# A linear-attention and GeGLU block on one core: output weights kept by head group, their packed copy made through DRAM on ScalarE's queue, and an epsilon column

## The chip, the cores and the metric

The kernel runs on one core of a Trainium2 chip. A core has five engines that take their instructions in order: TensorE (PE; its weight loads are shown apart, as PEld), VectorE (DVE), ScalarE (ACT), GpSimd (POOL) and SyncE (SP). Sixteen DMA engines move the data; an engine that issues a transfer puts it on its own queue, here SP's (q1 in the profile) and ACT's (q10). PE writes into PSUM, which has 8 banks of 128 x 512 f32.

The metric is the device time of one execution in microseconds (us). The kernel before takes 190.47 us, the median of 3 runs (190.45 to 190.97).

## The reference

The input x has 2048 tokens of D = 448. Linear attention with H = 16 heads of 28 is followed by a GeGLU with FF = 1792, both behind a layer norm without weights and with a residual:

```python
phi = lambda t: where(t > 0, t + 1, exp(t)) + 1e-6
q, k, v = split(layernorm(x) @ wqkv)          # 16 heads of 28
pq, pk  = phi(q), phi(k)
kv  = einsum("bhsd,bhse->bhde", pk, v)        # one 28 x 28 matrix for a head
z   = einsum("bhsd->bhd", pk)
den = einsum("bhqd,bhd->bhq", pq, z) + 1e-6
o   = einsum("bhqd,bhde->bhqe", pq, kv) / den[..., None]
h   = x + o @ wo
out = h + (gelu(layernorm(h) @ w_gate) * (layernorm(h) @ w_up)) @ w_down
```

All inputs and the output are bf16; gelu is the tanh form.

## The kernel before

**Tiles and stages.** The tokens are 16 tiles of 128, or 8 pairs of tiles. The stages, with their lines of the kernel before:

1. Layer norm of each tile (`xnn`), transposed to `xnT`: tiles 0 to 3 on PE, tiles 4 to 15 by DMA transposes `xT_4` to `xT_15` that SP issues (L455).
2. Projections `k_t` and `q_t`, 4 matmuls of 128x448 each (L469). For K: exp on ACT (`ek`, L480), phi on DVE, and sums over the tokens of phi(k) with the normed x (`pt`, L488). For Q: `eq_t` (exp, L496) and `rq_t` (relu, L497) on ACT, both reading the PSUM bank of the projection. Four PSUM banks go round for the projections, so a projection can start when the fourth projection before it has been read by both.
3. `kv` (16 matmuls, L527): the 448 x 448 matrix phi(k)^T v, of which a DVE operation (`kvm`, L531) keeps the 16 diagonal blocks of 28 x 28. The heads lie in 4 groups of 4 (112 channels). `w2_0` to `w2_3` (7 matmuls, L547) multiply this block-diagonal matrix with `wo`, so that the whole of attention behind phi(q) becomes one multiplication by `w2`, 448 x 448. The results are copied out by ACT (`evwA`) and DVE (`evwD`).
4. For each pair of tiles: phi(q) (`cq`, `aq`), `t1` = phi(q) times z (POOL), the sum over each head (`dr`, DVE), plus epsilon (`deA` for tiles 0 to 3, L574; `deP` for the later pairs, L588; ACT), reciprocal, and `pn`, the scaled phi(q). Pair 0 is transposed by PE (`tro`, L599) and copied by ACT (`evo_0`, `evo_1`, L602), pairs 1 to 7 by DMA transposes `oT_p` of SP (L605).
5. `out` = transposed phi(q) times `w2`. Pair 0 takes 4 matmuls a tile (`out1_0`, `out1_1`, L617). Pairs 1 to 7 run in two parts, `outA_p` and `outB_p` (L627, L628), as 7 steps, each of two matmuls of 64 rows that work side by side on two row halves of PE. One of the two needs `w2` with its row halves swapped: `w2s`, made by two transfers SBUF to SBUF, `dws0` and `dws1`, of 168 KB each, that SP issues.
6. Residual (`hr`, L633), layer norm (`ln2`, `rstd2`, on ACT for tiles 0 and 1) and `hn`, transposed by PE for pair 0 (`trh_0`, `trh_1`, L654, copied by ACT in `evhA_0`, L658, and by DVE), for later pairs by SP's DMA transposes.
7. `gu`: gate and up products (L731, L733), again 64 rows on each half of PE side by side. Tiles 0 and 1 go as 7 groups `gu2_0` to `gu2_6` of twice 256 columns, tiles 2 and 3 as `gu2_7` to `gu2_13`; tiles 4 to 15 go four at a time. The result of gate lies in PSUM banks 0 and 1 in turn, that of up in banks 6 and 7: `gu2_v` can start when gelu (`ge0`, `ge1`, ACT, L751) and the product (`hm0`, `hm1`, DVE, L753) of group v-2 have read theirs. Both work in halves of 256.
8. `down` (L697), the last residual, and the output.

ACT reads its functions from tables: exp, ln and relu from one, gelu from another. The kernel loads the second, `tbl2` (L762), behind the last exp, relu, ln and the copy `evhA_0`, and ahead of the first `ge`.

**What sets the order.** Every operation is put down as a task with the buffers that it reads and writes; from these come the waits. For each engine a row of the table `ORDERS` lists its tasks by number, and the engine issues them in just this order. A task whose wait isn't over holds up all that stands behind it on the same engine, a DMA issue too. A second table, `HOLD`, only says which of a task's waits stands first.

The gate and up weights come in four loads of SP, `dwg0`, `dwu0`, `dwg1`, `dwu1`, behind `xT_15`; the last of them is 64 x 7 x 1024, 896 KB.

## Time and profile before

| | |
|---|---|
| median of 3 runs | 190.47 us (190.45 to 190.97) |
| span of the profiled execution | 188.3 us |
| instructions | 4459 |
| granted PE clock | 1.000 |
| busy: PE, DVE, ACT, POOL | 184.3, 129.3, 76.5, 50.0 us |
| `kv` on PE | 35.96 to 36.99 us |
| load of the gelu table on ACT | 51.12 to 52.40 us |

How the views are to be read: the first part of the profile gives the busy time of each engine. A timeline row has the start, the length, the engine, the line, the operation, out<-in and its shape and a count of instructions that are taken together; a count of 2 on a row spans both and the gap between them. A row of windows has the start and end of a stretch, its length, the busy time and count of instructions of PE, PEld, DVE, ACT and POOL, the granted clock of PE, the share of the DMA engines' time, and GB/s. A row of waits has who waits, for what, the time in us, how often and the longest. Rows of DMA queues give packets, MB and the share of 16 engines' time. Times are us from the start of the span.

### The profile page before, as it was taken

Reading aid. Unit: us, or ns where it says so; the run is one execution under the profiler, and the core shown is the slowest. Engines: PE = TensorE matmul, PEld = TensorE weight load, DVE = VectorE, ACT = ScalarE, POOL = GpSimd, SP = SyncE. Lnnn points to the kernel's source line nnn. Section 1 sums busy time; section 2 is a strip of 40 time slices with the busy share of each in tenths; the row PEclk is TensorE's granted clock in tenths of the full one; section 3 lists DMA queues with packets and bytes.
Section 4 is the critical chain, followed back from the end, with each engine's and each line's share of the span. In section 5 each row is a group of like instructions: output and inputs, shape, how many; then the busy total and the mean of one; then the engine's idle time right before and its main releaser. Section 6 shows DMA issues by size and latency. Waiting matters only on the chain.

```text
span 188.3 us, 4459 instructions
## 1 busy us (share of the span) xinstructions
PE 184.3 (98%) x1813; PEld 109.2 (58%) x1813; DVE 129.3 (69%) x330; ACT 76.5 (41%) x220; POOL 50.0 (27%) x91
## 2 busy tenths in 40 slices
...
GB/s 169 387 231 88 96 104 194 218 222 174 65 320 64 95 52 116 84 52 0 0 3 98 144 54 0 0 3 2 3 135 111 3 0 24 3 0 98 3 79 140
DMA packets 35076, 17.11 MB, mean 91 GB/s; under 512 B 26864, under 2 KB 33648, under 8 KB 35056
## 3 DMA queue, kind: packets, MB, share of 16 engines
...
q10 hardware_dynamic: 624, 0.52, 0.8%
q8 instruction: 14, 0.23, 0.5%
q14 instruction: 6, 0.05, 0.1%
...
## 4 chain that ended last, share of the span: by engine, by line
PE 94%; DVE 3%; DMA 1%; issue 0%
PE ps L733 38%; PE ps L697 19%; PE ps L469 12%; PE ps L731 9%; PE ps L488 6%; PE ps L627 3%; PE ps L678 3%; PE ps L628 2%; DMA x_sb<-in_A_x_dram 1%; DVE st L413 1%; PE ps L617 1%; PE ps L547 1%; PE ps L527 1%; PE ps L443 0%; PE ps L654 0%; DVE den L572 0%
## 5 line engine op out<-in xcount | busy, mean ns | idle before, releaser
L733 PE MATMUL ps<-hnT,wgu_sb 64*128 64x512 bf16 (+1 forms) x490 | 88.8, 333 | 0.0
L731 PE MATMUL ps<-hnT,wgu_sb 64*128 64x512 bf16 (+1 forms) x490 | 88.6, 333 | 0.0
L751 ACT ACTIVATE gl<-ps 128x256 bf16<-128x256 f32 x112 | 36.6, 383 | 85.3 <-PE ps L731 84.4
L753 DVE TENSOR_TENSOR hh<-ps,gl 128x256 bf16<-128x256 f32 x112 | 42.1, 416 | 41.4 <-ACT gl L751 41.3
L733 PEld LDWEIGHTS ps<-hnT,wgu_sb 64*128 64x128 bf16 x490 | 45.2, 94 | 32.9 <-DVE hh L753 3.4
L731 PEld LDWEIGHTS ps<-hnT,wgu_sb 64*128 64x128 bf16 x490 | 45.4, 94 | 2.5
L697 PE MATMUL ps<-wd_sb,hh 64*128 64x448 bf16 x392 | 41.5, 349 | 0.0
L697 PEld LDWEIGHTS ps<-wd_sb,hh 64*128 64x128 bf16 x392 | 23.2, 94 | 14.5
L469 PE MATMUL ps<-wqk_sb,xnT 128*128 128x448 bf16 x128 | 27.4, 353 | 0.0
L413 DVE BATCH_NORM_STATS2 st<-x_sb 128x6 f32<-128x448 bf16 x32 | 19.2, 612 | 1.8 <-DMA x_sb<-in_A_x_dram 1.7
L585 POOL TENSOR_TENSOR t<-pq,zbc 128x448 f32<-128x448 bf16 x12 | 12.3, 1042 | 23.7 <-DVE pq L583 22.0
L469 PEld LDWEIGHTS ps<-wqk_sb,xnT 128*128 128x128 bf16 x128 | 11.9, 98 | 11.4 <-DVE pk L482 0.8
L488 PE MATMUL ps<-pk,xnn 128*128 128x448 bf16 x64 | 13.9, 352 | 0.0
L627 PE MATMUL ps<-w,pqnT 64*128 64x448 bf16 x49 | 11.5, 349 | 0.1
L425 POOL TENSOR_SCALAR ln<-mv 128x2 f32<-128x2 f32 x7 | 2.0, 291 | 35.2 <-DVE mv L414 35.0
L480 ACT ACTIVATE e<-ps 128x448 bf16<-128x448 f32 x16 | 8.5, 539 | 5.6 <-PE ps L469 5.5
L628 PE MATMUL ps<-pt_sb,pqnT 64*128 64x448 bf16 x42 | 10.2, 350 | 0.0
L633 DVE TENSOR_TENSOR x_sb<-ps,x_sb 128x448 bf16<-128x448 f32 x16 | 9.6, 616 | 0.7 <-PE ps L628 0.6
L662 POOL TENSOR_SCALAR hn<-x_sb,nm,rs 128x448 bf16<-128x448 bf16 x14 | 9.9, 719 | 0.4
L482 DVE SCALAR_TENSOR_TENSOR pk<-ps,e 128x448 bf16<-128x448 f32 x16 | 9.8, 617 | 0.1
L488 PEld LDWEIGHTS ps<-pk,xnn 128*128 128x128 bf16 x64 | 6.3, 98 | 5.9 <-DVE pk L482 0.3
L453 POOL TENSOR_SCALAR xnn<-x_sb,nm,rs 128x448 bf16<-128x448 bf16 x12 | 8.9, 744 | 2.2 <-ACT rs L422 1.9
...
## 6 DMA issues: line engine op xcount, KB each, us to landing
...
wgu_sb<-in_B_w_gate_dram SPq DMA_DIRECT2D x1, 896.0 KB, 12.1
wgu_sb<-in_B_w_up_dram SPq DMA_DIRECT2D x1, 896.0 KB, 16.5
...
```

The costliest lines, as they stand in the source:

```text
L413: op("dve", lambda e: e.bn_stats(st[:, t, :], src_ap), [b_src], [b_st[t]], "bnst%s_%d" % (tag, t))
L469: ins = e.matmul(ps[:, bk, 0:D], xnT[:, t, k, :], wqk_sb[:, k, c0:c0 + D], start=(k == 0), stop=(k == 3))
L488: ins = e.matmul(ps[:, BK_PT[c], 0:D], xnn[:, t % XN_R, c * 128:(c + 1) * 128], pk[:, ip, :], start=(t == 0), stop=(t == T - 1))
L585: op("pool", lambda e, n=n: e.tensor_tensor(t1[:, n, :], pq[:, a + n, :], zbc[:, :], ALU.mult), [b_pq[a + n]] + b_z, [b_t1[n]], "t1p_%d" % ...
L627: e.matmul(ps[:, BK_OUT[0], 0:D], pqnT[ra, i2, sg // 2, :], w2[ra, sg // 2, :], start=(sg == 0), stop=(sg == 5))
L628: ins = e.matmul(ps[:, BK_OUT[1], 0:D], pqnT[rb, i2, 3 + (sg + 1) // 2, :], (w2 if sg == 6 else w2s)[rb, sg // 2, :], start=(sg == 0), sto ...
L662: op("pool", lambda e, t=t, sh=sh: e.tensor_scalar(hn[:, sh, 0:D], x_sb[:, t, :], nm2[:, t:t + 1], rs2[:, t:t + 1], ALU.add, ALU.mult), [b ...
L697: ins = e.matmul(ps[:, bko[half][n], 0:D], hh[rows, j, sl[n]], wd_sb[rows, j, :], start=(j == 0 and (half == 0 or p == 6)), stop=(j == NJ ...
L731: first = e.matmul(psG[:, jj * N:(jj + 1) * N], wgu_sb[A_, k, j * 128:(j + 1) * 128], hnT[A_, ka_, c0:c0 + N], start=(k == 0), stop=(k == ...
L733: ins = e.matmul(psU[:, jj * N:(jj + 1) * N], wgu_sb[B_, k, j * 128:(j + 1) * 128], hnT[B_, kb_, c0:c0 + N], start=(k == 0), stop=(k == NK ...
L751: G.add("act", lambda e, gi=gi, cs_=cs_, psG=psG: e.activation(gl[:, gi, cs_], psG[:, cs_], AF.Gelu_apprx_tanh), r=[b_ps[BK_G[i]]], w=[b_g ...
L753: op("dve", lambda e, dst=dst, srcU=srcU, srcL=srcL: e.tensor_tensor(dst, srcU, srcL, ALU.mult), [b_ps[BK_U[i]], b_glh], [b_ar[j_][t % HR] ...
```

## The change

- `dwo`, the load of `wo`, stands on SP's queue behind `xT_5`, no longer ahead of `xT_4`.
- The block-diagonal matrix and its product are kept by head group: `w2g` has 112 rows in 4 groups, and `w2` takes 4 matmuls of 112x448 instead of 7 (after: L607). The zeroing of the wide buffer on POOL and the copy `kvd` on DVE (L536) are gone; the unused columns of `pqn` are zeroed by POOL for pair 1 too.
- Pair 1 is done as pair 0: `out1_2` and `out1_3`, 4 matmuls a tile (after: L675), in place of `outA_1` and `outB_1`. `oT_1` transposes 8 blocks of 128 instead of 7.
- Pairs 2 to 7 still run in two packed parts. Their weights `w2p` are a copy of `w2g` in which both row halves hold all of it. It is made through DRAM by three transfers of ScalarE's queue (after: L417): `dw2w` writes `w2g` to DRAM (`w_bounce`, 112x4x448, 392 KB), and `dw2r0` and `dw2r1` read it into the two row halves (64x7x448 each, 392 KB each, in the space of `pt_sb` and `wv_sb`). `dws0` and `dws1` are gone from SP.
- `t1` gets a 29th column per head that holds epsilon, so that the sum over 29 gives the denominator with epsilon. The 4 `deA` and 6 `deP` on ACT are gone.
- For each of the 14 groups `gu2`, gelu and product are one instruction of 512 columns (`geW`, `hmW`).
- `trh` waits for the two parts of `hn` apart.
- `ORDERS` and `HOLD` are new; of each a line stands in the diff.

On ACT, around the first layer norm behind attention: before, from `eq_11`,

```order
L496 ACTIVATE eq<-ps 128x448
L420 ACTIVATE ln<-mv,eps_t 128x1 x2
L422 ACTIVATE rs<-ln 128x1 x2
L497 ACTIVATE pq<-ps 128x448
L588 ACTIVATE den<-den,eps_d 128x32
L497 ACTIVATE pq<-ps 128x448
L496 ACTIVATE eq<-ps 128x448 x2
L497 ACTIVATE pq<-ps 128x448
L496 ACTIVATE eq<-ps 128x448
L658 ACTIVATE hnT<-ps 128x7x128
```

and now, also from `eq_11`; the two DMA rows are `dw2r0` and `dw2r1` (`pv_sb` holds `w2p`), and `rq_10` is the first `pq` row:

```order
L567 ACTIVATE eq<-ps 128x448
L491 ACTIVATE ln<-mv,eps_t 128x1
L417 DMA pv_sb<-w_bounce 64x7x448
L567 ACTIVATE eq<-ps 128x448
L493 ACTIVATE rs<-ln 128x1
L568 ACTIVATE pq<-ps 128x448
L491 ACTIVATE ln<-mv,eps_t 128x1
L493 ACTIVATE rs<-ln 128x1
L417 DMA pv_sb<-w_bounce 64x7x448
L568 ACTIVATE pq<-ps 128x448
L567 ACTIVATE eq<-ps 128x448
L717 ACTIVATE hnT<-ps 128x7x128
```

Two DMA issues have come in, `eq_10` and `rq_10` stand behind the first of them, and the epsilon row is gone. The write `dw2w` stands further ahead on the same engine, behind the copies of `w2` and `eq_7`:

```order
L568 ACTIVATE pq<-ps 128x448 x2
L610 ACTIVATE w2g<-ps 112x448 x2
L567 ACTIVATE eq<-ps 128x448
L417 DMA w_bounce<-w2g 112x4x448
L567 ACTIVATE eq<-ps 128x448
L660 ACTIVATE pqnT<-ps 128x512
```

On PE from `kv` to the transposes of the second layer norm: before,

```order
L527 MATMUL ps<-pt_sb,wv_sb 112x112 x16
L469 MATMUL ps<-wqk_sb,xnT 128x448 x8
L547 MATMUL ps<-wo_sb,hh 128x448 x6
L469 MATMUL ps<-wqk_sb,xnT 128x448 x4
L547 MATMUL ps<-wo_sb,hh 128x448
L599 MATMUL ps<-ident,pqn 128x128 x8
L469 MATMUL ps<-wqk_sb,xnT 128x448 x4
L617 MATMUL ps<-w,pqnT 128x448 x8
L469 MATMUL ps<-wqk_sb,xnT 128x448 x24
L654 MATMUL ps<-ident,hn 128x128 x14
```

and now:

```order
L598 MATMUL ps<-pv_sb 112x112 x16
L540 MATMUL ps<-wqk_sb,xnT 128x448 x4
L607 MATMUL ps<-wo_sb,hh 112x448 x4
L540 MATMUL ps<-wqk_sb,xnT 128x448 x4
L657 MATMUL ps<-ident,pqn 128x128 x4
L540 MATMUL ps<-wqk_sb,xnT 128x448 x8
L657 MATMUL ps<-ident,pqn 128x128 x4
L675 MATMUL ps<-w2g,pqnT 128x448 x4
L540 MATMUL ps<-wqk_sb,xnT 128x448 x4
L675 MATMUL ps<-w2g,pqnT 128x448 x4
L540 MATMUL ps<-wqk_sb,xnT 128x448 x20
L713 MATMUL ps<-ident,hn 128x128 x14
```

One projection (4 matmuls, `q_7`) instead of two stands between `kv` and `w2`, and the transposes and output products of pair 0 are spread among the projections. The last projections are now, in this order, `q_12`, `q_10`, `q_13`, `q_15`, `q_14`.

The diff, cut to what the tasks do:

```diff
--- before.py
+++ after.py
...
-    " 168 179 192 180 346 193 205 218 307 219 206 234 308 347 235 250 251 349 309 290 289 310 311 313 293 315 317"
+    " 167 168 179 192 180 344 193 205 218 307 219 206 234 308 345 235 250 251 347 309 290 289 310 311 293 313 314"
...
-    66: (36,), 141: (140,), 165: (164,), 214: (213,), 216: (215,), 323: (302,), 326: (324,), 431: (340,), 704:
+    435: (434,), 436: (435,), 437: (433,), 438: (437,), 439: (438,), 440: (436,), 441: (440,), 442: (441,),
...
-        wv_sb = sb("wv_sb", [128, 4, D], BF16)
+        pv_sb = sb("pv_sb", [128, 8, D], BF16)
+        pt_sb, wv_sb, w2p = pv_sb[:, 0:4, :], pv_sb[:, 4:8, :], pv_sb[:, 0:NK, :]
...
-        pt_sb = sb("pt_sb", [128, 4, D], BF16)
         zbc = sb("zbc", [128, D], F32)
-        w2 = sb("w2", [128, 4, D], BF16)
-        t1 = sb("t1", [128, 2, D], F32)
+        w2g = sb("w2g", [GW, NG, D], BF16)
+        w2d = nc.dram_tensor("w2_bounce", [D, D], BF16)
+        t1 = sb("t1", [128, 2, H, DH + 1], F32)
         den = sb("den", [128, 4, H], F32)
-        eps_d = sb("eps_d", [128, 1], F32)
...
-        kvz = hh[0:GW, 6:9, :].rearrange("p a b -> p (a b)")
-        w2s = pt_sb[:, 0:3, :]
+        t1f = t1[:].rearrange("p n h d -> p n (h d)")[:, :, 0:D]
+        kvz = hh[0:GW, 6, 0:D]
...
-        dma_x("sp", 12, 16)
+        tx12 = dma_x("sp", 12, 16)
         dma_w3("sp", wv_sb, 2 * D, 3 * D, b_wv, "dwv")
         dma_w1("sp", wv_sb, 2 * D, 3 * D, b_wv, "dwv_t")
         two = dma("sp", wo_sb[:, :, :], A_wo.rearrange("(g p) n -> p g n", p=GW), [b_wo], "dwo")
...
-        op("pool", lambda e: e.memset(eps_d[:], EPS), [], [b_epsd], "epsd")
+        op("pool", lambda e: e.memset(t1[:, :, :, DH:DH + 1], EPS), [], [b_epsd], "epsd")
...
-        op("pool", lambda e: e.memset(pqn[:, 0, :].rearrange("p (n c) -> p n c", n=2)[:, :, D:512], 0.0), [], b_pqn[0], "pqnpad")
-        op("pool", lambda e: e.memset(kvz[:, GW:15 * GW], 0.0), [], [b_kvm], "kvzpad")
+        for i_ in range(2):
+            op("pool", lambda e, i_=i_: e.memset(pqn[:, i_, :].rearrange("p (n g c) -> p n g c", n=2, g=NG)[:, :, :, GW:128], 0.0), [], b_pqn[i_], "pqnpad_%d" % i_)
...
-                G.add("sp", lambda e: e.dma_start_transpose(xnT[:, t, :, :], xnn[:, i, :]), r=[b_xn[i], b_ones2], w=b_xnT[t], name="xT_%d" % t, kind="dma", after=[two])
+                G.add("sp", lambda e: e.dma_start_transpose(xnT[:, t, :, :], xnn[:, i, :]), r=[b_xn[i], b_ones2], w=b_xnT[t], name="xT_%d" % t, kind="dma", after=[tx12])
...
-        for c in range(4):
-            def fw2(e, c=c):
-                gs = (c, c + 1) if c < 3 else (3,)
-                ins = None
-                for g in gs:
-                    ins = e.matmul(ps[:, BK_W2[c], 0:D], kvc(g, c), wo_sb[:, g, :], start=(g == gs[0]), stop=(g == gs[-1]))
-                return ins
-            G.add("pe", fw2, r=[b_kvm, b_wo] + ([b_kvd] if c == 3 else []), w=[b_ps[BK_W2[c]]], name="w2_%d" % c)
...
+        for g in range(NG):
+            G.add("pe", lambda e, g=g: e.matmul(ps[0:GW, BK_W2[g], 0:D], kvz[:, g * GW:(g + 1) * GW], wo_sb[:, g, :], start=True, stop=True),
+                  r=[b_kvm, b_wo], w=[b_ps[BK_W2[g]]], name="w2_%d" % g)
+            if g % 2 == 0:
...
-        for h, (to, of) in enumerate(((A_, B_), (B_, A_))):
-            dma("sp", w2s[to, :, :], w2[of, 0:3, :], [b_w2s[h]], "dws%d" % h, r=b_w2[0:3], after=xts[-1:])
+                op("dve", lambda e, g=g: e.tensor_copy(w2g[:, g, :], ps[0:GW, BK_W2[g], 0:D]), [b_ps[BK_W2[g]]], [b_w2[g]], "evwD_%d" % g)
+        dma("act", w2d.ap().rearrange("(g p) n -> p g n", p=GW), w2g[:, :, :], [b_w2d], "dw2w", r=b_w2)
+        for h, rows in enumerate((A_, B_)):
+            dma("act", w2p[rows, :, :], w2d.ap().rearrange("(k p) n -> p k n", p=64), [b_w2p[h]], "dw2r%d" % h, r=[b_w2d])
...
-                    op(eng, lambda e, t=t, n=n: e.tensor_tensor(t1[:, n, :], pq[:, t, :], zbc[:, :], ALU.mult), [b_pq[t]] + b_z, [b_t1[n]], "t1%s_%d" % (eng[0], t))
+                    op(eng, lambda e, t=t, n=n: e.tensor_tensor(t1[:, n, :, 0:DH], pq[:, t, :].rearrange("p (h d) -> p h d", h=H), zbc[:, :].rearrange("p (h d) -> p h d", h=H), ALU.mult), [b_pq[t]] + b_z, [b_t1[n]], "t1%s_%d" % (eng[0], t))
...
-                    op("dve", lambda e, n=n, i=i: e.tensor_reduce(den[:, i, :], t1[:, n, :].rearrange("p (h d) -> p h d", h=H), AX.X, ALU.add),
-                       [b_t1[n]], [b_den[i]], "dr_%d" % t)
-                    op("act", lambda e, i=i: e.activation(den[:, i, :], den[:, i, :], AF.Identity, bias=eps_d[:, 0:1]), [b_den[i], b_epsd], [b_den[i]], "deA_%d" % t)
+                    op("dve", lambda e, n=n, i=i: e.tensor_reduce(den[:, i, :], t1[:, n, :, :], AX.X, ALU.add),
+                       [b_t1[n], b_epsd], [b_den[i]], "dr_%d" % t)
...
-                    op("dve", lambda e, t=t, n=n, i=i, i2=i2: e.tensor_tensor(
-                        pqn[:, i2, n * pst:n * pst + D].rearrange("p (h d) -> p h d", h=H), pq[:, t, :].rearrange("p (h d) -> p h d", h=H),
-                        rd[:, i, :].unsqueeze(2).to_broadcast([128, H, DH]), ALU.mult),
+                    dst = pqn[:, i2, n * 512:n * 512 + 512].rearrange("p (g c) -> p g c", g=NG)[:, :, 0:GW]
+                    op("dve", lambda e, t=t, i=i, dst=dst: e.tensor_tensor(
+                        dst.rearrange("p g (h d) -> p g h d", d=DH), pq[:, t, :].rearrange("p (g h d) -> p g h d", g=NG, d=DH),
+                        rd[:, i, :].rearrange("p (g h) -> p g h", g=NG).unsqueeze(3).to_broadcast([128, NG, 4, DH]), ALU.mult),
                        [b_pq[t], b_rd[i]], [b_pqn[i2][n]], "pn_%d" % t)
...
-                op("dve", lambda e: e.tensor_reduce(den[:, i:i + 2, :].rearrange("p n h -> p (n h)"), t1[:, :, :].rearrange("p n (h d) -> p (n h) d", h=H), AX.X, ALU.add),
-                   b_t1, b_den[i:i + 2], "drP_%d" % p)
-                op("act", lambda e: e.activation(den[:, i:i + 2, :], den[:, i:i + 2, :], AF.Identity, bias=eps_d[:, 0:1]), b_den[i:i + 2] + [b_epsd], b_den[i:i + 2], "deP_%d" % p)
+                    op("pool", lambda e, n=n: e.tensor_tensor(t1[:, n, :, 0:DH], pq[:, a + n, :].rearrange("p (h d) -> p h d", h=H), zbc[:, :].rearrange("p (h d) -> p h d", h=H), ALU.mult), [b_pq[a + n]] + b_z, [b_t1[n]], "t1p_%d" % (a + n))
+                op("dve", lambda e: e.tensor_reduce(den[:, i:i + 2, :].rearrange("p n h -> p (n h)"), t1[:, :, :, :].rearrange("p n h d -> p (n h) d"), AX.X, ALU.add),
+                   b_t1 + [b_epsd], b_den[i:i + 2], "drP_%d" % p)
...
-                G.add("sp", lambda e, i2=i2: e.dma_start_transpose(pqnT[:, i2, 0:NK, :], pqn[:, i2, 0:2 * D]),
+                G.add("sp", lambda e, i2=i2: e.dma_start_transpose(pqnT[:, i2, 0:8 if p == 1 else NK, :], pqn[:, i2, 0:1024 if p == 1 else 2 * D]),
...
-            if p == 0:
+            if p < 2:
...
-                            e.matmul(ps[:, BK_OUT[0], 0:D], pqnT[ra, i2, sg // 2, :], w2[ra, sg // 2, :], start=(sg == 0), stop=(sg == 5))
-                            ins = e.matmul(ps[:, BK_OUT[1], 0:D], pqnT[rb, i2, 3 + (sg + 1) // 2, :], (w2 if sg == 6 else w2s)[rb, sg // 2, :], start=(sg == 0), stop=(sg == 5))
+                            e.matmul(ps[:, BK_OUT[0], 0:D], pqnT[ra, i2, sg // 2, :], w2p[ra, sg, :], start=(sg == 0), stop=(sg == 5))
+                            ins = e.matmul(ps[:, BK_OUT[1], 0:D], pqnT[rb, i2, 3 + (sg + 1) // 2, :], w2p[rb, sg, :], start=(sg == 0), stop=(sg == 5))
                         return ins
-                    parts.append(G.add("pe", foutp, r=b_pqnT[i2] + b_w2 + b_w2s, w=[b_ps[b_] for b_ in BK_OUT], name="out%s_%d" % (part, p), sync=parts[-1:]))
+                    parts.append(G.add("pe", foutp, r=b_pqnT[i2] + b_w2p, w=[b_ps[b_] for b_ in BK_OUT], name="out%s_%d" % (part, p), sync=parts[-1:]))
...
+                        for m, k in enumerate((0, 1, 2, 4, 5, 6, 3)):
+                            W(m)
...
+                    G.add("pe", ftrh, r=[(b_hn[sh], 0), (b_hnd[sh], 6), (b_ident, 0)], w=[(b_ps[BK_TH[t]], 0)], name="trh_%d" % t, mw=True)
...
-                for hh_ in range(2):
-                    cs_ = slice(hh_ * 256, (hh_ + 1) * 256)
+                for hh_ in range(2 if nj == 1 else 1):
+                    cs_ = slice(hh_ * 256, (hh_ + 1) * 256) if nj == 1 else slice(0, 512)
...
-                    b_glh = b_gl2[gi][hh_]
+                    b_glh = b_gl2[gi][hh_:] if nj > 1 else b_gl2[gi][hh_:hh_ + 1]
                     G.add("act", lambda e, gi=gi, cs_=cs_, psG=psG: e.activation(gl[:, gi, cs_], psG[:, cs_], AF.Gelu_apprx_tanh),
-                          r=[b_ps[BK_G[i]]], w=[b_glh], name="ge%d_%d" % (hh_, v), after=[tbl2])
+                          r=[b_ps[BK_G[i]]], w=b_glh, name="ge%s%d_%d" % ("W" if nj > 1 else "", hh_, v), after=[tbl2])
                     op("dve", lambda e, dst=dst, srcU=srcU, srcL=srcL: e.tensor_tensor(dst, srcU, srcL, ALU.mult),
-                       [b_ps[BK_U[i]], b_glh], [b_ar[j_][t % HR] for j_ in jr for t in th], "hm%d_%d" % (hh_, v))
+                       [b_ps[BK_U[i]]] + b_glh, [b_ar[j_][t % HR] for j_ in jr for t in th], "hm%s%d_%d" % ("W" if nj > 1 else "", hh_, v))
```

31 lines of the change are left out of this document (9 added, 22 removed), and 130 rows, old and new, of tables (HOLD, ORDERS).

## The prediction

> **What bounds the kernel now.** I read the page first: the busy times, then the chain of work that ended last.
>
> ```profile
> span 188.3 us, 4459 instructions
> PE 184.3 (98%) x1813; PEld 109.2 (58%) x1813; DVE 129.3 (69%) x330; ACT 76.5 (41%) x220; POOL 50.0 (27%) x91
> ...
> PE 94%; DVE 3%; DMA 1%; issue 0%
> ```
>
> PE is busy for 184.3 of 188.3 us, so the end moves by two things only: PE work that is added or taken away, and stretches in which PE waits. The profiled span of 188.3 us stands 2.2 us under the median of 190.47; I make the sum as a difference on the span's times and add it to the median.
>
> Next I read the windows around the change, since the busy share of ACT over the whole span (41%) hides one stage. A row has start and end, length, busy time and count of PE, PEld, DVE, ACT and POOL, clock, DMA share, GB/s.
>
> ```profile
> 35.40:52.40 17.00, 16.88 (x152) 10.16 (x152) 16.28 (x38) 16.55 (x40) 6.88 (x8) 1.00 0.87 167
> 54.00:66.00 12.00, 12.00 (x190) 9.86 (x189) 11.87 (x33) 3.35 (x11) 6.10 (x10) 1.00 0.52 130
> ```
>
> From 35.4 to 52.4 us ACT is busy for 16.55 of 17.00 us: there it has no room, and PE (16.88) has none either. From 54 us on ACT has plenty, and PE is gapless. So what the change does to the time is settled by one handover, which the timelines show (ACT, then DVE, then PE):
>
> ```profile
> 45.39 0.49 ACT L420 ACTIVATE ln<-mv,eps_t 128x1 f32<-128x1 f32 x2
> ...
> 46.02 0.53 ACT L497 ACTIVATE pq<-ps 128x448 bf16<-128x448 f32 x1
> 46.45 0.31 ACT L588 ACTIVATE den<-den,eps_d 128x32 f32<-128x32 f32 x1
> 46.66 0.53 ACT L497 ACTIVATE pq<-ps 128x448 bf16<-128x448 f32 x1
> ...
> 48.84 0.95 ACT L658 ACTIVATE hnT<-ps 128x896 bf16<-128x896 bf16 x1
> ...
> 51.12 1.28 ACT L762 ACT_TABLE_LOAD   x1
> 52.41 0.66 ACT L751 ACTIVATE gl<-ps 128x256 bf16<-128x256 f32 x2
> ...
> 53.10 0.76 DVE L753 TENSOR_TENSOR hh<-ps,gl 128x256 bf16<-128x256 f32 x2
> ...
> 53.95 0.27 PE L733 MATMUL ps<-hnT,wgu_sb 64*128 64x256 bf16 x1
> ```
>
> ACT runs without a gap through the last projections to the gelu table; gelu starts at 52.41, the product ends at 53.86, and `gu2_2`, which needs that PSUM bank, starts at 53.95. ACT's chain is therefore just in time: whatever makes the table load later makes `gu2_2` later, and everything behind it. In the new order `outB_2` stands ahead of `gu2_2`, 3 packed steps of 0.19 (49.56 to 50.14 in the PE rows below). The same place in the program is then 53.95 + 0.57 = 54.52 us; that is the mark against which I measure.
>
> **The change: PE's work.** The rows are PE's, with one DVE row among them.
>
> ```profile
> 34.23 1.68 PE L469 MATMUL ps<-wqk_sb,xnT 128*128 128x448 bf16 x8
> 35.96 1.03 PE L527 MATMUL ps<-pt_sb,wv_sb 128*112 128x112 bf16 x16
> 36.83 1.68 PE L469 MATMUL ps<-wqk_sb,xnT 128*128 128x448 bf16 x8
> 37.19 0.61 DVE L531 TENSOR_TENSOR hh<-ps,mask 112x448 bf16<-112x448 f32 x1
> 38.34 1.30 PE L547 MATMUL ps<-wo_sb,hh 112*128 112x448 bf16 x6
> ...
> 47.69 0.94 PE L654 MATMUL ps<-ident,hn 128*128 128x128 bf16 x14
> ...
> 49.14 0.35 PE L627 MATMUL ps<-w,pqnT 64*128 64x448 bf16 x1
> 49.56 0.36 PE L627 MATMUL ps<-w,pqnT 64*128 64x448 bf16 x1
> ...
> 50.14 0.27 PE L733 MATMUL ps<-hnT,wgu_sb 64*128 64x256 bf16 x1
> ...
> 51.67 0.27 PE L733 MATMUL ps<-hnT,wgu_sb 64*128 64x256 bf16 x1
> ```
>
> Eight projection matmuls take from 36.83 to 38.34, 0.19 each; the lengths overlap. Three `w2` matmuls fall out: -0.57. Pair 1 goes from 7 packed steps of 0.19 to 8 matmuls of 0.19: +0.19. Sum -0.38. The gap between 49.14 and 49.56, 0.42 instead of 0.19, is a wait of 0.23 of `outB_1` that can vanish with it. Against that, `kvm` ends at 37.80 and only `q_7` (0.76, to 37.59) now covers it, not two projections: PE waits 0.2 to 0.3. PE alone therefore stands at -0.6 to -0.1. This counts only if ACT isn't the later one.
>
> **ACT's work.** Four `deA` and one `deP` ahead of the table load fall out. One takes 0.21 of ACT's time (46.45 to 46.66, where the next starts): -1.05. The five later `deP` lie in ACT's idle time, nothing. Three DMA issues come in. ACT's own issues in this trace are at the start, and the one with as many rows as the new ones (448 of 896 bytes) is SP's load of `wo`:
>
> ```profile
> 0.80 0.42 ACTq L346 DMA_DIRECT2D x_sb<-in_A_x_dram  x1
> 1.25 1.01 ACTq L346 DMA_DIRECT2D wqk_sb<-in_A_wqkv_dram  x2
> 5.50 0.59 SPq L346 DMA_DIRECT2D wo_sb<-in_A_wo_dram  x1
> ```
>
> So 0.42 to 0.6 each; I take 0.6, by the like size: +1.8. The merged gelu and product are priced from 256 and 448 columns of the same engines:
>
> ```profile
> L751 ACT ACTIVATE gl<-ps 128x256 bf16<-128x256 f32 x112 | 36.6, 383 | 85.3 <-PE ps L731 84.4
> L753 DVE TENSOR_TENSOR hh<-ps,gl 128x256 bf16<-128x256 f32 x112 | 42.1, 416 | 41.4 <-ACT gl L751 41.3
> L480 ACT ACTIVATE e<-ps 128x448 bf16<-128x448 f32 x16 | 8.5, 539 | 5.6 <-PE ps L469 5.5
> L482 DVE SCALAR_TENSOR_TENSOR pk<-ps,e 128x448 bf16<-128x448 f32 x16 | 9.8, 617 | 0.1
> ```
>
> ACT: 0.539 + 64/192 of 0.156 = 0.59; DVE: 0.617 + 64/192 of 0.201 = 0.68. With 0.1 for the handovers, 1.4 us from the table to `gu2_2`, against 1.54 before: -0.15. In steady state one bank's round is 1.4 to 1.55 against 1.53 for the other bank's group (50.14 to 51.67), so small waits of 0.1 in all may come; DVE's saving is hidden by PE. Without any wait ACT's chain would so come out at -1.05 + 1.8 - 0.15 = +0.6 against 53.95, that is 54.55, as good as the mark.
>
> **The wait that is added.** `dw2r0` reads what `dw2w` has written, so ACT stands at its issue until the write has landed, and behind it stand `eq_10`, `rstd2_0`, `rq_10`, the whole rest of the exp stage, and the table. PE waits too: `q_14` uses the PSUM bank of `q_10`. DVE waits for `rstd2` in `hn`, and `pnP_2` and SP's `oT_2` stand behind that. The question is when `dw2w` lands.
>
> `dw2w` is issued once the copies of `w2` are done, about 40 us (before: SP issues `dws0`, which waits for the same copies, at 40.37). At that time the DMA engines are full with the last weights:
>
> ```profile
> 29.33 0.76 SPq L346 DMA_DIRECT2D wgu_sb<-in_B_w_up_dram  x1
> wgu_sb<-in_B_w_up_dram SPq DMA_DIRECT2D x1, 896.0 KB, 16.5
> 40.37 1.16 SPq L346 DMA_DIRECT2D pt_sb<-w  x2
> pt_sb<-w SPq DMA_DIRECT2D x2, 168.0 KB, 5.7
> ...
> q1 hardware_dynamic: 318, 0.65, 105.4%
> ```
>
> The last load lands at 29.33 + 16.5 = 45.8; the last row (stretch 40 to 43 us) shows all 16 engines busy with SP's queue. The two copies `dws`, on that same queue, took 5.7 us and landed at 46.1 to 46.5. Would ACT's queue be served sooner? The start of the kernel has both queues loaded at once; the first two rows are 3.7 to 4.6 us, the last two 4.6 to 5.3:
>
> ```profile
> q10 hardware_dynamic: 317, 0.28, 89.8%
> q1 hardware_dynamic: 45, 0.05, 17.1%
> ...
> q1 hardware_dynamic: 238, 0.21, 87.1%
> q10 hardware_dynamic: 69, 0.05, 21.3%
> ```
>
> There ACT's load (q10, issued 1.25) moves almost alone, and then SP's (q1, issued later) almost alone: the transfers go nearly whole, in the order of issue. By this `dw2w` comes behind the last load. `dws`, 336 KB, ended 0.7 after it; 392 KB take 0.82: landing at L = 46.65. Ends: 42.1 if ACT's queue goes first (about 40 us, 0.6 for the issue, 1.05 at the rate of the start, 0.5 for the landing), and 47.3 if the write runs into `oT_1` as well. I take 46.65, since it rests on the nearest rows, same time and same kind.
>
> ACT reaches `dw2r0` at: before's 45.39 - 0.84 (`deA`) + 0.6 (`dw2w`) - 0.43 (`eq_10`, `rq_10` moved behind, `rq_11` ahead) + 0.16 (`ln2_0`; two `ln` and two `rs` take 45.39 to 46.02) = 44.9. It waits 1.75 us.
>
> From L the chain to the table's end is: `dw2r0` 0.6, `eq_10` 0.43 (46.02 to 46.45), `rstd2_0` 0.16, `rq_10` 0.43, `ln2_1` and `rstd2_1` 0.32, `dw2r1` 0.6, `rq_15` and `eq_15` 0.86, `evhA_0` 0.85 (0.95 less the 0.1 by which such rows overlap), six more of `eq` and `rq` 2.58, table 1.29 (51.12 to 52.41): 8.1. Plus 1.4: `gu2_2` at L + 9.5. PE's own chain from there is as long: `q_14` at L + 1.7, then 0.76, `trh` 0.88 (47.69 to 49.14 less three steps), 8 x 0.19, two groups 3.06, 7 x 0.19: L + 9.25. So the change is L + 9.5 - 54.52 = L - 45.0, with L = 46.65 some +1.65 us, and from then on all of PE is later by this: 190.47 + 1.65 = **192.1 us**. What PE saves lies ahead of this wait, or beside it, and is lost in it.
>
> Small things: the load of `wo` behind `xT_5` lets two transposes leave earlier by its issue (0.59) and the ten others up to as much later, -0.6 to +0.6 if PE stood on them throughout; PE's busy share leaves little for that, and I take nothing. POOL loses one zeroing and gains one, far ahead; nothing. `dw2r0` and `dw2r1` have from about 47 and 49 to 54 us, enough for 392 KB; `wd`, 1568 KB, is issued behind `oT_2` and so behind both.
>
> **A rule against the rows.** The start-up windows above show transfers nearly whole, in order of issue. The Trainium skill, "DMA: Bandwidth & Descriptors", section "Queues, rings and completion order", says that each DMA engine takes turns between the queues for which it has work, a packet of some 9 to 17 descriptors at a time. By that rule, as an estimate, `dw2w` (28 rows an engine) would need two or three turns, each behind one of the 28 rows an engine of the last load, and land well ahead of that load's end or just with it.
>
> **The rivals.**
>
> 1. The two queues take turns. In 3.7 to 4.6 us SP's queue still moved 45 packets beside ACT's 317, which speaks a little for it. `dw2w` then shares the engines with the last load, whose 0.9 MB take 4.2 us at the 0.65 MB in 3 us of the row above. Two turns of half of that, from 40 us, plus 1.05 for itself put L at 45.3 (one turn and the landing: 44; end of the load: 46.2): L - 45.0 = +0.3, 190.8.
> 2. `dw2w` is in time. ACT's queue is served at once, L = 42.1, below the 44.9 at which ACT comes; no wait, the chain is at 54.55: no change, 190.5.
> 3. Faster. As 2, and an issue costs ACT 0.42, not 0.6: then ACT's chain ends at 54.0, PE is the later one, and its -0.6 to -0.1 show; with the 0.2 that PE waits ahead of `kv` (34.23 + 8 x 0.19 to 35.96) at most -0.8: 189.7 to 190.4, taken as 189.8. It decides from L under 44.9 and issues under 0.45 each. Against it stand the 5.7 us of `dws` in the same stretch.
> 4. The change does other than it says: the wait of `trh`, the later `xT_6` or the weights of `outA_2` cost more than I see, with `dw2w` in time: up to +1, 191.3.
>
> **How the numbers follow.** Stuck behind the last load 0.55 (192.1; L from 46.0 to 47.3 gives 191.5 to 192.8, and with 0.3 for small waits in the merged groups 193.1); turns 0.17, half of it within the bound; in time without effect 0.13; faster 0.12; other 0.03. What this measurement can tell from no change is about 0.3%, 0.57 us: faster is under 189.90, slower over 191.04. So faster 0.12, same 0.13 + 0.09 = 0.22, slower 0.55 + 0.08 + 0.03 = 0.66. The range of 8 in 10 reaches from 190.1, with the turns and most of the no-wait case in it, to 193.1; the likeliest case alone has 191.5 to 193.1.
>
> **What would show it.** In the profile after: ACT idle ahead of `dw2r0` or of `eq_10`, about 44.9 to 46.7, put down to the transfer into `w_bounce`; that transfer's landing, 6 to 7 us after its issue; a PE wait of 1 us or more at `q_14`; the table load at about L + 6.8 = 53.5 instead of 51.12; gapless PE from `gu2_3` on. I'm wrong if `w_bounce` lands by 44.9, or if the table load starts by 52, or if PE waits anew further back, at `outA_2` or in the groups with the merged gelu.

## The result and the profile after

The changed kernel takes 192.48 us (median of 6 runs, 192.06 to 193.45), the kernel before 190.75 us beside it (190.45 to 190.97). The ratio is 1.0096, 95% interval 1.0076 to 1.0117: about 1.8 us slower. The ratios and times of the experiments below leave out eight executions, in four of the runs, that had a granted clock of 0.983 to 0.991 and took over 1.5% more than the fastest of their kernel.

The page of the changed kernel:

```profile
span 190.9 us, 4399 instructions
PE 184.8 (97%) x1804; PEld 113.0 (59%) x1804; DVE 128.8 (67%) x315; ACT 73.2 (38%) x196; POOL 49.6 (26%) x91
...
PE 81%; DVE 9%; DMA 7%; SPq 1%; ACT 1%; issue 0%; ACTq 0%
```

ACT has lost 3.3 us of work and DVE 0.5, and neither helps: PE is still the one that is always busy. But of the chain that ended last PE now makes up 81%, not 94%; 13% have gone to DVE, DMA and ACT. That is the form that new waits of PE take in the chain. The profiled execution of the changed kernel took 192.61 us, 1.7 us more than its span. In 58 executions of the kernel before that were run beside the experiments, the time was 1.93 to 2.06 us more than the span, and those with a span of 188.3 took 190.28 to 190.33. So by estimate the execution of before that was profiled took about 190.3, some 0.4 less than the median of before. (Why the changed kernel has 0.2 us less outside its span isn't shown.) So the two spans differ by 2.6 us where the medians differ by 1.7; the events in the traces are to be compared with that in mind.

The chain of the changed kernel (start, length, what), in the stretch of the handover:

```profile
39.99 1.17 DVE w2g L612 x2
41.18 6.34 DMA w_bounce<-w2g
...
47.55 0.62 ACTq L417
...
48.22 0.54 ACT eq L567
...
49.34 0.93 PE ps L540 x4
```

This is the wait that was added, read in one go: the copies of `w2g` end, `dw2w` is issued at 41.18 and lands 6.34 us later, at 47.52; only then ACT issues `dw2r0` (47.55), then come `eq_10` and `rq_10`, and only then PE starts `q_14`. The timelines of ACT, DVE and PE for the same place:

```profile
46.48 0.29 ACT L491 ACTIVATE ln<-mv,eps_t 128x1 f32<-128x1 f32 x1 [0.33 <-DVE mv L485]
47.55 0.62 ACTq L417 DMA_DIRECT2D pv_sb<-w_bounce  x1
48.22 0.54 ACT L567 ACTIVATE eq<-ps 128x448 bf16<-128x448 f32 x1 [1.44 <-PE ps L540]
...
54.56 1.28 ACT L821 ACT_TABLE_LOAD   x1
55.85 1.08 ACT L810 ACTIVATE gl<-ps 128x512 bf16<-128x512 f32 x2
...
56.48 0.69 DVE L812 TENSOR_TENSOR hh<-ps,gl 128x512 bf16<-128x512 f32 x1 [0.36 <-ACT gl L810]
...
57.13 0.27 PE L790 MATMUL ps<-hnT,wgu_sb 64*128 64x256 bf16 x1
```

One row can mislead: ACT's 1.44 us of idle time ahead of `eq_10` are put down to PE (L540). `q_10` was done at about 46.8 (PE starts its last projections at 45.17 with `q_12`, then `q_10`, 0.76 each). The time is `dw2r0`'s: ACT ended `ln2_0` at 46.77, stood until 47.55, and took 0.62 for the issue, which isn't counted as busy. The waits of PE name the right one:

```profile
PEld ps L540 <- ACT pq L568: 1.4, 1, 1.4
...
PEld ps L607 <- DVE hh L602: 0.9, 1, 0.9
```

The second of these is the wait for `kvm`. The table load stands at 54.56, where before had it at 51.12, and `gu2_2` starts at 57.13, where the mark of the prediction was 54.52: 2.6 us later, the whole difference of the spans. From there on the two kernels run alike.

Two places ahead of the handover have changed too. First the load of `wo` on SP's queue; the first two rows are SP's timeline, the third is the DMA issue of `xT_6` with its time to landing (4.1 us in the kernel before), the last is PE's `k_6`:

```profile
13.45 0.58 SPq L417 DMA_DIRECT2D wo_sb<-in_A_wo_dram  x1
14.09 14.46 SPq L526 DMA_TRANSPOSE xnT<-xnn  x10
...
xnT<-xnn SPq DMA_TRANSPOSE x1, 4.6
...
18.84 0.92 PE L540 MATMUL ps<-wqk_sb,xnT 128*128 128x448 bf16 x4 [0.59 <-DVE mv L485]
```

`xT_6` is issued at 14.09 and lands at 18.7, and `k_6` starts at 18.84. (The row names a DVE operation; `k_6` waits for `xT_6` and for `pk_4`, and `pk_4` was over.) From 14.09 on SP issues transposes without a gap: `xT_15` is issued 1.3 us later than before, the last weight load 1.3 us later (30.64, not 29.33), and `kv` starts at 37.12, not 35.96. Not all of that is the load's: `xT_4`, which stands ahead of it, is issued 0.5 us later already (10.81, not 10.31); in the other runs it is issued at 10.32 to 10.69, wherever `wo` stands.

Second, `kvm`, in the rows of PE and DVE:

```profile
37.12 0.99 PE L598 MATMUL ps<-pv_sb 128*112 128x112 bf16 x16
37.95 0.92 PE L540 MATMUL ps<-wqk_sb,xnT 128*128 128x448 bf16 x4
39.37 0.96 PE L607 MATMUL ps<-wo_sb,hh 112*112 112x448 bf16 x4 [0.50 <-DVE hh L602]
...
37.88 0.91 DVE L635 TENSOR_TENSOR pqn<-pq,rd 128x448 bf16<-128x448 bf16 x1
38.70 0.61 DVE L602 TENSOR_TENSOR hh<-ps,mask 112x448 bf16<-112x448 f32 x1
```

`kv` is done at 38.1, but DVE is in `pn_0` until 38.79 and does `kvm` behind it; PE is through with `q_7` at 38.7 and starts `w2` at 39.37, 0.67 us later than without a wait.

### The profile page after: what moved, and what is told of

It is laid out like the page before. It is cut to its first block, busy times and chain, and to the rows that moved or that the text cites. A ratio compares the mean times of both kernels' runs of the same rounds, so it can differ in the third digit from the quotient of the medians.

```text
span 190.9 us, 4399 instructions
## 1 busy us (share of the span) xinstructions
PE 184.8 (97%) x1804; PEld 113.0 (59%) x1804; DVE 128.8 (67%) x315; ACT 73.2 (38%) x196; POOL 49.6 (26%) x91
## 4 chain that ended last, share of the span: by engine, by line
PE 81%; DVE 9%; DMA 7%; SPq 1%; ACT 1%; issue 0%; ACTq 0%
PE ps L792 40%; PE ps L756 19%; PE ps L790 6%; PE ps L540 5%; PE ps L559 4%; DMA w_bounce<-w2g 3%; DMA x_sb<-in_A_x_dram 3%; PE ps L737 3%; DVE st L484 3%; PE ps L685 2%; PE ps L686 1%; DVE pk L553 1%; PE ps L675 1%; SPq L417 1%; DVE w2g L612 1%; DVE e L552 1%
## 5 line engine op out<-in xcount | busy, mean ns | idle before, releaser
L810 ACT ACTIVATE gl<-ps 128x256 bf16<-128x256 f32 (+1 forms) x98 | 35.3, 414 | 87.1 <-PE ps L790 86.2
L812 DVE TENSOR_TENSOR hh<-ps,gl 128x256 bf16<-128x256 f32 (+1 forms) x98 | 41.0, 455 | 40.7 <-ACT gl L810 40.7
L790 PEld LDWEIGHTS ps<-hnT,wgu_sb 64*128 64x128 bf16 x490 | 45.2, 94 | 2.8 <-ACT eq L567 0.4
L756 PEld LDWEIGHTS ps<-wd_sb,hh 64*128 64x128 bf16 x392 | 25.5, 94 | 12.1
L540 PE MATMUL ps<-wqk_sb,xnT 128*128 128x448 bf16 x128 | 28.1, 353 | 1.8 <-ACT pq L568 1.0
L540 PEld LDWEIGHTS ps<-wqk_sb,xnT 128*128 128x128 bf16 x128 | 11.9, 98 | 14.2 <-ACT pq L568 1.4
L644 POOL TENSOR_TENSOR t<-pq,zbc 128x448 f32<-128x448 bf16 x12 | 12.9, 1090 | 27.0 <-DVE pq L642 27.0
L721 POOL TENSOR_SCALAR hn<-x_sb,nm,rs 128x448 bf16<-128x448 bf16 x14 | 10.8, 780 | 0.5
L685 PE MATMUL ps<-pv_sb,pqnT 64*128 64x448 bf16 x42 | 9.9, 349 | 0.1
L686 PE MATMUL ps<-pv_sb,pqnT 64*128 64x448 bf16 x42 | 9.9, 349 | 0.0
```

The source lines that it names most:

```text
L540: ins = e.matmul(ps[:, bk, 0:D], xnT[:, t, k, :], wqk_sb[:, k, c0:c0 + D], start=(k == 0), stop=(k == 3))
L644: op("pool", lambda e, n=n: e.tensor_tensor(t1[:, n, :, 0:DH], pq[:, a + n, :].rearrange("p (h d) -> p h d", h=H), zbc[:, :].rearrange("p ...
L685: e.matmul(ps[:, BK_OUT[0], 0:D], pqnT[ra, i2, sg // 2, :], w2p[ra, sg, :], start=(sg == 0), stop=(sg == 5))
L686: ins = e.matmul(ps[:, BK_OUT[1], 0:D], pqnT[rb, i2, 3 + (sg + 1) // 2, :], w2p[rb, sg, :], start=(sg == 0), stop=(sg == 5))
L756: ins = e.matmul(ps[:, bko[half][n], 0:D], hh[rows, j, sl[n]], wd_sb[rows, j, :], start=(j == 0 and (half == 0 or p == 6)), stop=(j == NJ ...
L790: first = e.matmul(psG[:, jj * N:(jj + 1) * N], wgu_sb[A_, k, j * 128:(j + 1) * 128], hnT[A_, ka_, c0:c0 + N], start=(k == 0), stop=(k == ...
```

## The experiments

Theory A: ScalarE stands at `dw2r0` until `dw2w` has landed, which it does only behind the last weight load; what counts at the end is that landing, L. The rivals: the waits simply add up (B); the added issues and the merged gelu cost the time (C); the write is slow by itself (D). "Both edits" below is the run with `wo` back and the reads on SP.

| edit (of the changed kernel, if not said otherwise) | ratio to before | 95% interval | L | PE waits over 0.3 us from 15 us on (profiled execution) |
|---|---|---|---|---|
| none | 1.0096 | 1.0076 to 1.0117 | 47.5 | `k_6` 0.75, `kvm` 0.67, `q_14` 1.1 |
| `wo` back | 1.0059 | 1.0042 to 1.0077 | 46.9 | `kvm` 0.67, `q_14` 1.6 |
| reads on SP | 1.0049 | 1.0026 to 1.0071 | 46.7 | `k_6` 0.35, `kvm` 0.67 |
| both | 1.0003 | 0.9988 to 1.0018 | 47.1 | `kvm` 0.67, `outA_2` 0.9 |
| last load behind `oT_1` | 1.0278 | 1.0227 to 1.0330 | 45.2 | `k_6` 2.2, `kvm` 0.67, `outA_2` 3.3 |
| reads later on ACT, `wo` back | 1.0169 | 1.0129 to 1.0208 | 46.5 | `kvm` 0.67, `outA_2` 2.4 |
| before, with `wo` late | 1.0045 | 1.0025 to 1.0064 | - | `k_6` 0.68 |

What L hangs on shows across the runs. In ten profiled executions the last load lay ahead of `dw2w` in the queues (the changed kernel and nine of its versions, the later ones below among them). In all ten L came 1.09 to 1.19 us behind the landing of that load, though `dw2w` was issued at anything from 39.9 to 41.2 us.

**The load of `wo` back ahead of `xT_4`.**

```diff
 # SP's row of ORDERS; 14 is dwo, 98 and 113 are xT_4 and xT_5
-    "... 12 13 98 113 14 128 ..."
+    "... 12 13 14 98 113 128 ..."
```

> The changed kernel with the load of wo back ahead of xT_4; all else as changed. Theory A (ScalarE stands at dw2r0 until dw2w has landed, dw2w lands behind the last weight load, and only that landing counts): the last load lands about 0.5 us earlier (45.8 instead of 46.4), dw2w at 47.0 instead of 47.5, so the kernel is 0.5 us faster than the changed one, 1.2 to 1.3 us slower than before (ratio 1.007); the projections and kv come 1.2 us earlier and PE's wait at q_14 grows from 1.1 to about 1.8 us. Rival B (the waits add up, each given back in full when its cause goes): 1.2 us faster than the changed kernel, ratio about 1.003, the wait at q_14 stays 1.1 us.

Measured: 191.71 us, ratio 1.0059 (1.0042 to 1.0077), 0.7 us less than the changed kernel. The wait at `k_6` is gone, `kv` starts at 36.0, 1.1 us earlier, and about 0.4 us of that comes to nothing, because ACT now stands longer. ACT's rows and the wait of PE:

```profile
45.35 0.29 ACT L491 ACTIVATE ln<-mv,eps_t 128x1 f32<-128x1 f32 x1 [0.32 <-DVE mv L485]
46.88 0.64 ACTq L417 DMA_DIRECT2D pv_sb<-w_bounce  x1
...
PEld ps L540 <- ACT pq L568: 1.9, 1, 1.9
```

ACT is at `dw2r0` at 45.6 and stands until 46.88, 1.2 us instead of 0.8. The last load lands at 45.7 instead of 46.4, and L moves by 0.66 us, as the time does (0.7). In both kernels the table load stands 7.0 us behind L (at 54.56 and 53.91). The wait at `q_14` goes from 1.1 to 1.6. That is theory A; B's 1.2 us aren't there.

**The two reads on SP.**

```diff
-            dma("act", w2p[rows, :, :], ...)
+            dma("sp", w2p[rows, :, :], ...)
 # ORDERS: 305 and 306 (dw2r0, dw2r1) out of ACT's row; SP's row, behind oT_1:
-    "... 287 356 382 357 ..."
+    "... 287 356 305 306 382 357 ..."
```

> The changed kernel with dw2r0 and dw2r1 issued by SP behind oT_1 instead of by ScalarE; dw2w stays on ScalarE. Theory A: dw2w still lands at 47.5, but ScalarE doesn't stand there; the wait at q_14 goes and the table load starts about 1.5 us earlier. What is left is kv 1.2 us late and 0.5 us of wait for kvm, less 0.6 us of PE work and of the wait of outB_1: 0.7 to 1.1 us faster than the changed kernel, ratio 1.004 to 1.006. Rival C (the time comes from the added work on ScalarE and the merged gelu, not from the wait): no change against the changed kernel, ratio 1.009. If SP's own standing at the reads makes oT_2 late, PE waits at outA_2.

Measured: 191.54 us, ratio 1.0049 (1.0026 to 1.0071), 0.9 us less than the changed kernel, as theory A expected, where C expected no change. But the edit takes two issues (0.62 and 0.58 us) off ACT as well as the standing, so this run alone doesn't part the two; the run with the reads later on ScalarE does. In the windows from 45 to 50 us, the changed kernel and then this one (columns as in the prediction):

```profile
45.00:50.00 5.00, 4.02 (x22) 1.93 (x21) 4.33 (x11) 2.90 (x9) 1.20 (x1) 1.00 0.69 170
```

```profile
45.00:50.00 5.00, 5.00 (x38) 2.85 (x36) 5.00 (x14) 4.29 (x12) 0.32 (x1) 1.00 0.75 169
```

PE is busy for all of the 5 us. `dw2w` landed 0.9 us sooner here (46.66), but that is not the reason: 7.0 us behind L would put the table load at 53.7, and it stands at 52.27. ACT's chain no longer hangs on the landing. (This execution took 190.71 us, 0.8 us less than the median of its run.)

**Both edits.**

> Both edits: the load of wo back ahead of xT_4, and dw2r0 and dw2r1 issued by SP behind oT_1. Theory A: no wait on ScalarE and kv as early as before; left are 0.5 us for kvm against 0.6 us of PE work and wait that fall out: -0.5 to +0.2 us against before, ratio 0.997 to 1.001. Rival C: still 0.5 us or more slower than before.

Measured: 190.68 us against 190.60, ratio 1.0003 (0.9988 to 1.0018): the 1.8 us are gone, and the two parts (0.7 and 0.9) make up nearly all of them. What stays are the 0.67 of `kvm`, and in the profiled execution a new wait of 0.9 us at `outA_2`, for `oT_2`. That execution took 191.36 us, as long as any of the twelve; in the run with gelu in halves below, whose loads and reads stand in the same places, `oT_2` landed at 53.31 instead of 54.02 and PE didn't wait for it. The DMA issue of `oT_2` in this run, and in the changed kernel:

```profile
pqnT<-pqn SPq DMA_TRANSPOSE x1, 4.7
```

```profile
pqnT<-pqn SPq DMA_TRANSPOSE x1, 3.2
```

It is now issued at 49.29, with both reads of 392 KB under way (they land at 51.35 and 53.14), and takes 1.5 us longer than in the changed kernel, where it was issued at 51.37, just ahead of the first read's landing (51.82; the second landed at 53.49).

**The last weight load behind `oT_1`.**

```diff
 # SP's row: 287 (dwu1) behind 356 (oT_1)
-    "... 284 285 286 287 356 382 ..."
+    "... 284 285 286 356 287 382 ..."
```

> The changed kernel with the last weight load (dwu1) issued behind oT_1 on SP, so that it isn't under way when dw2w is issued; reads stay on ScalarE. Theory A with transfers going nearly whole in order of issue: dw2w lands right behind the load before it (41.8) and itself, at 42.5 to 43.5, ScalarE comes to dw2r0 later than that and doesn't stand; 0.7 to 1.1 us faster than the changed kernel as in the run with the reads on SP, ratio 1.004 to 1.006, unless dwu1 (then landing at 51 to 53) makes gu2_3 wait. Rival D (dw2w's time is that of a write to DRAM and back, not of the load ahead): it takes 5 us or more all the same, and the time doesn't change.

Measured: 196.07 us (194.55 to 197.32 in three executions), ratio 1.0278 (1.0227 to 1.0330), against all theories. The profile parts the two questions. The write of `w2g` was faster:

```profile
w_bounce<-w2g ACTq DMA_DIRECT2D x1, 392.0 KB, 3.1
...
PE ps L685 <- DMA pqnT<-pqn: 3.2, 1, 3.2
```

3.1 us from issue to landing with no load ahead, not 6.3: D falls, and ACT didn't stand at `dw2r0`. But the last load (issued at 47.6) now shares the DMA engines with the two reads and `oT_2`; `dw2r1` lands at 57.7, `oT_2` at 58.5, and PE waits 3.3 us at `outA_2`. The profiled execution took 197.54 us at a granted clock of 0.991, where all other profiled executions had 1.000. It had a wait of 2.2 us at `k_6`, where the other runs with `wo` behind `xT_5` had 0.35 to 0.75, and behind PE's wait at `outA_2` its clock fell, as two windows show (the third number from the end is the clock):

```profile
59.00:61.00 2.00, 1.94 (x18) 0.86 (x16) 0.12 (x1) 0.00 (x0) 0.00 (x0) 0.77 1.07 369
61.00:63.00 2.00, 2.00 (x24) 1.37 (x20) 0.50 (x1) 0.00 (x0) 0.00 (x0) 0.50 1.82 290
```

With 0.88 from 63 to 65 us, that cost PE 1.7 us by estimate, beyond the wait itself. Not every wait of this length did that: in the run with pair 2 by groups below, the clock stayed at 1.000 behind a wait of 3.4 us.

**The reads later on ScalarE, `wo` back.**

```diff
 # ACT's row, by the names of the tasks
-    ... ln2_0 dw2r0 eq_10 rstd2_0 rq_10 ln2_1 rstd2_1 dw2r1 rq_15 eq_15 evhA_0 eq_12 ...
+    ... ln2_0 eq_10 rstd2_0 rq_10 ln2_1 rstd2_1 rq_15 eq_15 evhA_0 dw2r0 dw2r1 eq_12 ...
```

> The changed kernel with the load of wo back, and with dw2r0 and dw2r1 still on ScalarE's queue but behind evhA_0 in its order, where ScalarE comes at about 48.9 us, after dw2w has landed (46.6 to 47.5). Theory A: the 1.6 us at q_14 go; the two issues (1.2 us) still lengthen ScalarE's chain, and the reads land at 53 to 55 us, so PE waits about 1 us at outA_2 or gu2_2: ratio 1.001 to 1.005 against 1.006 with the reads where they were. If the two transfers cost by being on ScalarE's queue at all, wherever they stand: 1.006 or more.

Measured: 194.19 us, ratio 1.0169 (1.0129 to 1.0208). The wait at `q_14` is gone, as theory A had it, but the time is worse than with it: the reads are issued at 48.3 and 49.0, `oT_2` at 49.1, and it lands only at 55.3, `dw2r1` at 54.6. PE waits at `outA_2` until 55.50 (the row names the second read, which lands ahead of `oT_2`):

```profile
PEld ps L685 <- DMA pv_sb<-w_bounce: 2.4, 1, 2.4
```

The expectation had the wait in the right place and at less than half its size. Of the six executions two, the profiled one among them, had a granted clock of 1.000 and took 192.56 and 192.86 us; the other four had 0.991 and took 194.2 to 195.0. So the trace accounts for about half of the loss; what the four lost besides isn't shown.

The trace also answers what the run with the reads on SP left open, by ACT's table load:

```profile
52.39 1.28 ACT L821 ACT_TABLE_LOAD   x1
```

With `wo` back and the reads where they were it stood at 53.91; here, with the same two issues still on ACT, at 52.39; with both edits, at 52.01. So by estimate some 1.5 us of the difference are the standing and 0.4 the issues: C has a small part.

**The kernel before, with the load of `wo` behind `xT_5` alone.**

```diff
 # SP's row of before
-    "... 12 13 14 98 113 128 ..."
+    "... 12 13 98 113 14 128 ..."
-        dma_x("sp", 12, 16)
+        tx12 = dma_x("sp", 12, 16)
-    ... name="xT_%d" % t, kind="dma", after=[two])
+    ... name="xT_%d" % t, kind="dma", after=[tx12])
```

> The kernel before with one edit: the load of wo behind xT_5 instead of ahead of xT_4. Theory A': the load makes the transposes behind it later, kv comes 0.5 to 1.2 us later and, since ScalarE and PE have no room from there to the gelu table, all of it reaches the end: 0.5 to 1.2 us slower than before (ratio 1.003 to 1.006), with the single times further apart than those of before. Rival (my prediction's own term: nothing): ratio 0.999 to 1.001.

Measured: 191.32 us, ratio 1.0045 (1.0025 to 1.0064), 0.7 to 0.9 us slower, single times from 191.1 to 192.5. The wait of 0.68 us at `k_6` is the one new wait of PE. So this one line of the change costs 0.7 to 0.9 us, in either kernel.

**`q_8` ahead of `w2` (both edits besides).**

```diff
 # PE's row, by the names of the tasks
-    kv q_7 w2_2 w2_1 w2_0 w2_3 q_6 tro_0 q_9 q_8 tro_1 out1_0 ...
+    kv q_7 q_8 w2_2 w2_1 w2_0 w2_3 q_6 tro_0 q_9 tro_1 out1_0 ...
```

> The run with both edits (load of wo back, reads on SP) and q_8 ahead of the w2 matmuls on PE again. If the wait for kvm (0.67 us there against none before) is a cost of its own: 0.4 us faster than that run, ratio 0.998. If what sets the end there is oT_2, which lands at 54.0 us behind the two reads in the DMA engines and holds outA_2 for 0.9 us: no change, ratio 1.000, and the wait at outA_2 grows by what PE has gained.

Measured: 191.40 us, ratio 1.0039 (1.0021 to 1.0057): not faster than both edits alone but 0.7 us slower. The wait for `kvm` is gone, and PE waits at the next places instead:

```profile
41.66 0.93 PE L675 MATMUL ps<-w2g,pqnT 112*128 112x448 bf16 x4 [0.37 <-ACT pqnT L660]
```

that is 0.54 at `out1_0` for `evo_0` by the spacing of the matmuls, 0.2 at `trh`, and 1.0 at `outA_2`; L is 47.5. L is 0.4 us later than with both edits, though `dw2w` was issued only 0.15 us later; most of it is the landing of the last load (46.30, not 45.96), and why that came later isn't shown.

**The epsilon column undone (both edits besides).**

```diff
-    op("pool", lambda e: e.memset(t1[:, :, :, DH:DH + 1], EPS), ...)
+    op("pool", lambda e: e.memset(eps_d[:], EPS), ...)
-    e.tensor_reduce(den[:, i, :], t1[:, n, :, :], AX.X, ALU.add)
+    e.tensor_reduce(den[:, i, :], t1[:, n, :, 0:DH], AX.X, ALU.add)
+    op("act", lambda e, i=i: e.activation(den[:, i, :], den[:, i, :], AF.Identity, bias=eps_d[:, 0:1]), ..., "deA_%d" % t)
 # and the same for the pairs, deP
```

> The run with both edits, without the epsilon column: the 4 deA and 6 deP are back on ScalarE and the sum goes over 28. By my sum ScalarE's chain to the gelu table gets 1.05 us longer (five at 0.21), and DVE's reciprocals wait for ScalarE again: table load at 53.0 instead of 52.0, 0.5 to 1.2 us slower than the run with both edits, ratio 1.003 to 1.006. If the column is worth nothing: the same.

Measured: 194.09 us, ratio 1.0182 (1.0163 to 1.0202), 3.4 us slower than both edits, about three times the most that was expected. The trace has two parts of it: 1.5 us at `q_14` and `trh`, and one wait of 1.95 us at 71 us, where a `deP` stands behind a gelu and DVE's reciprocal behind it:

```profile
DVE rd L650 <- ACT den L649: 3.1, 2, 2.6
...
PE ps L795 <- DVE hh L815: 1.8, 1, 1.8
```

The second part comes from the place that I gave `deP_4` in ACT's row, and says nothing of the column. The first is near the 1.05 us of the sum, but it holds DVE's waits for ACT as well.

**The epsilon column alone, in the kernel before.**

```diff
-        t1 = sb("t1", [128, 2, D], F32)
+        t1 = sb("t1", [128, 2, H, DH + 1], F32)
 # deA and deP gone; the sums go over 29
```

> The kernel before with the epsilon column alone: no deA and deP, the sum goes over 29. By my sum ScalarE's chain to the gelu table gets 1.05 us shorter (table load at about 50.1 instead of 51.1), but PE was only just in time there and doesn't wait in before's trace but for 0.2 us ahead of kv and 0.2 us ahead of outB_1: nothing to gain but those, ratio 0.997 to 1.000. If ScalarE was the one that set the pace ahead of gu2_2 rather than PE, 0.5 us or more faster: ratio under 0.997.

Measured: 190.70 us, ratio 1.0014 (0.9998 to 1.0029): nothing gained. ACT's row of the table load:

```profile
51.36 1.28 ACT L760 ACT_TABLE_LOAD   x1
```

It hasn't moved to 50.1. With less work ACT waits for PE's projections (0.9 us ahead of one `eq`), which come no sooner.

**Gelu and product in halves (both edits besides).**

```diff
-                for hh_ in range(2 if nj == 1 else 1):
+                for hh_ in range(2):
-                        njh = nj
+                        njh = nj // 2
```

> The run with both edits, with gelu and product of the 14 first groups in halves of 256 again. By my sum the first product ends 0.15 us later and nothing else changes, since PE is the later one in the groups: within 0.2 us of the run with both edits, ratio 0.999 to 1.002. If merged instructions made PE wait for a bank in each group, the halves are faster by 0.1 us or more a group, 1 us in all.

Measured: 190.99 us, ratio 1.0019 (1.0005 to 1.0032); both edits had 1.0003 (0.9988 to 1.0018), so the merged form is about 0.3 us ahead, at the edge of what the intervals tell apart. It makes PE wait nowhere in the groups.

**Pair 2 by head group as well (both edits besides), without and with `q_8` ahead of `w2`.**

```diff
-            if p < 2:
+            if p < 3:
                 for n in range(2):
                     def fout(e, W, n=n):
 # pnP_2 writes the layout by groups, oT_2 transposes 8 blocks;
 # SP's row: oT_1 oT_2 dw2r0 dw2r1 dwd
```

> The run with both edits, and pair 2 done by head group as well (out1_4 and out1_5, 8 matmuls in place of outA_2 and outB_2), so that the packed copy is first needed by outA_3 at about 60 us; the two reads stand behind oT_2 on SP. No chain now hangs on the landing of dw2w. Theory A: the wait of up to 1 us at outA_2 goes for 0.19 us more PE work; PE's wait for kvm (0.67) stays: ratio 0.997 to 1.001, single times closer together than with both edits alone. If the reads cost by the DMA engines' time itself, hT or wd come late and PE waits anew behind 60 us.

> The same with q_8 ahead of the w2 matmuls, q_11 ahead of out1_0, and rq_8 between the two copies of w2 on ScalarE, so that neither kvm nor evo_0 is waited for. Theory A: PE's 0.67 and the 0.54 that the run with q_8 first showed at out1_0 go: 0.3 to 0.6 us faster than the run with pair 2 by groups, ratio 0.995 to 0.998. If ScalarE's chain to the gelu table is the later one, the gain shows up again as a wait at gu2_2: ratio 0.998 to 1.000.

Measured: 192.84 us, ratio 1.0102 (1.0078 to 1.0125), and 192.53 us, 1.0109 (1.0080 to 1.0138). The two aren't told apart, both are far from the ratios that theory A gave, and the single times of the first (192.3 to 194.0) lie further apart than with both edits alone, not closer. Nothing waits at pair 2 any longer, as expected, and `kvm` isn't waited for in the second. But the reads now stand ahead of the load of `wd` (1568 KB) and of `oT_3`:

```profile
PEld ps L690 <- DMA pqnT<-pqn: 3.5, 1, 3.5
```

`oT_3` lands at 64.5 us (59.2 in the kernel before), and PE waits 3.4 us at `outA_3`, 1.5 in the second run. This is the case that the expectation named last: the reads cost by the DMA engines' time. Neither version, nor any other that was run, beats the kernel before.

## Why the prediction was right

Forecast was 192.1 us in a range of 190.1 to 193.1, and slower; measured 192.48. The mechanism is the forecast one: `dw2w` lands behind the last weight load, ACT stands at `dw2r0`, PE at `q_14`, and `gu2_2` comes late. Point by point:

- **From the landing to `gu2_2`.** Forecast L + 9.5; measured 57.13 - 47.52 = 9.6. The table load was forecast at L + 6.8 and came at L + 7.0.
- **The landing.** Forecast 46.65, measured 47.52. Of the 0.87, 0.5 are the last load's own landing (46.36 instead of 45.84), and the rest is that L came 1.17 us behind it, not 0.82. Whether the load of `wo` pushed the last load isn't shown: with `wo` back that load landed at 45.74 and L is 46.86, but with `wo` late and the reads on SP it landed at 45.49, and with `wo` early in the other versions at 45.28 to 46.30. `dw2w` took 6.3 us from its issue, where 6 to 7 were forecast. The bound of 42.1 for L gave the write alone 2.1 us, with 0.5 for its landing that no row showed; the run with the last load behind `oT_1` shows 3.1.
- **The queues.** The forecast went by whole transfers in the order of issue. The landing bears out the price of that. The DMA queues in the stretch from 42 to 43 us and, in the other two rows, from 45 to 46:

```profile
q1 hardware_dynamic: 103, 0.21, 104.8%
```

```profile
q10 hardware_dynamic: 349, 0.31, 98.4%
q1 hardware_dynamic: 11, 0.01, 5.2%
```

  `dw2w` was issued at 41.18 on q10. In 42 to 43 us no packet of q10 moves, and the first one moves at 44.33; by then all but 45 of the last load's 448 rows have gone. Rival 1, by which the queues take turns, is out as it was priced (L at 45.3). Turns as such are not. The Trainium skill ("DMA: Bandwidth & Descriptors", "Queues, rings and completion order") has each engine take turns between the queues for which it has work, a packet of some 9 to 17 descriptors at a time. With nothing ahead (the run with the last load behind `oT_1`) the first packet of `dw2w` moved 0.88 us after its issue. Here that would be 42.06, and from then on the last load had 279 rows left, by estimate 17 for each of the 16 engines; with `wo` back and with both edits it had 19 and 21. One turn of the page's size, or little more, is as long as that. So the traces don't tell whole transfers from turns so coarse; the prediction's estimate by that rule counted with all 28 rows an engine of the load, and these 17 to 21 were left.
- **How long ACT stands.** Forecast 1.75 us, measured 0.8. ACT came to `dw2r0` at 46.8, not 44.9, since `kv` was 1.2 us late and ACT waited for PE and DVE on the way. It changes nothing, since the landing sets the end; with `wo` back ACT stood 1.2 us.
- **The load of `wo`: the term that was mis-sized.** The prediction put it among the small things and took nothing. It cost 0.7 to 0.9 us by itself (1.0045), and taking it back gave 0.7 us. The working had bounds of -0.6 to +0.6 and dropped them with the remark that PE's busy share leaves little; that says nothing of a wait that is yet to come. In the kernel before with `wo` late, `xT_6` was issued 0.4 us later and landed 0.9 us later, and PE waited 0.68 us at `k_6`; from there to `kv` PE has no gap in which to make that up, and `kv` came 0.9 us later.
- **`kvm`.** Forecast 0.2 to 0.3, measured 0.67. The working took `kvm` to follow `kv` at once; in DVE's new order it stands behind `pn_0`. The bound of -0.6 for PE alone left this wait out (-0.38, -0.23 and +0.2 make -0.4), and the wait of 0.23 that was to vanish is still there, 0.22 us at `outB_2`.
- **ACT's sum without the wait.** The 1.05 us that the epsilon column saves were counted as a shorter way to the table. Alone in the kernel before they didn't bring the table load forward (51.36 instead of 51.12) and gained nothing: ACT was full there but paced by PE. The three issues cost 0.35, 0.62 and 0.58 us where 0.6 each were taken. The merged gelu and product were priced at 0.59 and 0.68; the mean of the first ten after is 0.60 and 0.68.
- **The size.** 1.65 us forecast, 1.7 to 1.8 measured. That they lie so close is in part luck. In the traces `gu2_2` came 2.6 us behind the mark, 0.9 more than forecast, since L was 0.87 later. The times differ by less than the traces: the profiled execution of before, from which the mark of 54.52 comes, was by estimate 0.4 us ahead of before's median, that of the changed kernel 0.13 behind its own, and the changed kernel has 0.2 us less outside its span.
- **"`dw2r0` and `dw2r1` have time enough".** True in the changed kernel, where the wait that holds up ACT also holds up `oT_2` until the reads are nearly through. In most versions that took the wait away, `oT_2` or `oT_3` ran into the reads: `oT_2` took 3.8 to 6.2 us from issue to landing, `oT_3` 6.2 and 8.1 with pair 2 by groups, against 3.0 and 2.9 in the kernel before. With the reads on SP alone and with gelu in halves PE still didn't wait for it.
